# Experts taken by the rank of their counts, one set of split weights for both parts, and routing in larger groups

## The chip, the cores and the metric

The kernel runs on one core of one Trainium2 chip. The metric is the device time in microseconds (us) of one execution; the times of an unchanged kernel are the median of a few runs, lowest and highest beside it.

## What is computed

Three stages follow one another on 3,072 tokens of 384 values (4 sequences of 768, 8 heads of 48):

```
scan:  S_re, S_im = a * S + k v^T  (complex gate a, |a| < 1);  y[t] = q[t] S_re
moe:   logits = x @ w_gate + softplus(x @ w_noise) * noise          # 8 experts
       top2 of the logits, shares = softmax over the two
       out[token] += share * relu(x[token] @ w1[e]) @ w2[e]          # w1 384x1024, w2 1024x384
mlp:   h = max(x @ u1, x @ u2, x @ u3);  out = h @ w_out             # u 384x768, w_out 768x384
```

Inputs and outputs are float32. How many tokens an expert gets depends on the inputs; the mean is 2 x 3,072 / 8 = 768.

## The kernel before, in words

**Scan.** The tokens are 24 chunks of 128, in 6 levels of time step with one chunk of each of the 4 sequences. For each chunk PE builds scores (L732), DVE multiplies them with a mask (L736, two products a chunk), PE makes the chunk's output and state (L750, L753, L771), and the gating matmuls (L809) give the logits. A chunk's output is kept as two float16 halves (`xhl`).

**Routing.** `route()` (L822 on) takes the chunks in 12 groups of 2 (`groups` in the table `P`, L43). For a group DVE finds the two best experts of each token (L844 to L866), PE and DVE turn one-hot rows into a slot in the expert's list (L882 to L900), POOL adds up the counts (L870), and four small instructions make the softmax shares (L907 to L916). Then POOL scatters the chunk's rows, one indirect DMA for each chunk and choice (L940, each with a one-element memset ahead of it, L939), into `xs_rows`, where every expert has a region of its own.

**Experts.** An expert's weights come from memory in 7 pieces (3 of w1, 4 of w2) and are split into float16 high and low halves, the high one on ACT (L985), the low one on DVE (L987), so that three float16 matmuls stand for one in float32. Each expert is done twice. The first pass (L1023 on; matmuls L1037 and L1057) takes its first 384 rows, which come from the first 12 chunks, so that it can run while the scan is still going on; `bump` (L1197) pads every expert's count to 384 there. The second pass (L1076 on; matmuls L1098, L1124) takes rows 384 to 816 (`CAP` = 816), which is three tiles of 128 rows and one of 48; the tile of 48 is done as pairs of half tiles (L1131). The first passes go through experts 0 to 7, the second ones back from 7 to 0, and only expert 7 uses the same split weights in both, so weights are fetched and split 15 times. Results go to `ys_rows` and, of the first pass, to `yf_rows` too. Rows past 816 of an expert would be done by a block under a condition at run time (L1442 on).

**Final stage.** The rows of a token's two experts are gathered by indirect DMA (L1507), weighed and added (L1513), and go through the last three-way layer (L1557) and the output layer (L1583). The first tokens' combination starts earlier, from `yf_rows` (`combine_first`, L1340 on; gathers L1351, transposes L1376 and its neighbours).

**What sets the order.** All work up to the final stage is entered into a list scheduler, `Order` (L68 on), with for each operation its engines and cost, what it reads and writes, the buffers it holds, and a due time (chunk or part number plus a value of the table `o`, L36 on). Its greedy loop writes all instructions out in the order that it finds, so a change of a cost or of a number in `o` can move any instruction. SP issues the loads, the transposing loads of the experts' rows (L1006, one for each 128 columns of a half), the weight pieces (L997) and the writes of results (L1069, L1152). On every engine instructions run in the order in which they stand.

Of the kernel before, what the change touches and what calls it, by code (L numbers as in the profile page):

```python
# [22 lines left out]
SX = 2.0 ** 5  # L23
# [12 lines left out]
    o=dict(load=-278.44, e1=-80.82, g=-44.76, ex=27.33, lam=13.6, t1=124.93, t2=491.73, f=-344.44, sin=58.57,  # L36
           tc=-621.27, qkv=204.29, v=669.22, a0=-227.64, a=84.82, b=-227.33, d=-609.19, c=-58.23, s=-165.23,
           l=90.33, f_=14.8, rt=-247.65, scat=-246.48, zf=803.51, gate=-153.95, noise=149.71, xw=125.96, xx=-312.17,
           x1=-201.57, xe=-424.5, x2=17.72, xo=-1189.75, yw=61.09, yx=-118.02, y1=-594.47, ye=185.57, y2=-134.08,
           yo=454.95, uw=1011.11, ue=388.46, pl=276.27, z=-83.6, mr=971.2),  # L40
    sets=[4, 4, 4, 4, 4, 4],
    e1ph=[0, 1, 2, 3, 4, 5],
    groups=[2, 2, 2, 2, 2, 2, 2, 2, 2, 2, 2, 2],  # L43
# [205 lines left out]
def tile_kernel(ctx, tc, q, k, v, a_re, a_im, w_gate, w_noise, noise, w1, w2,  # L249
# [20 lines left out]

    xs = nc.dram_tensor("xs_rows", (E * NT, 2 * HD), F16).ap()

    NX = -(-((E - 2) * RA - (E * CAP - 2 * NT)) // 128) * 128
# [5 lines left out]
    zs = nc.dram_tensor("z_rows", (NT, 2 * HD), F16).ap()  # L279

# [107 lines left out]
    for nm, pool_, shape, dt in (  # L388
# [15 lines left out]
            ("rw", ck, [128, 61 * max(P["groups"])], F32),  # L404
# [415 lines left out]
    RW = (("e", E), ("nl", E), ("mx", 8), ("ix", 8), ("oh0", E), ("oh1", E), ("rb", E), ("dm", 2), ("ew", 2), ("sm", 1))  # L820

    def route(gi, i0, n):  # L822
# [6 lines left out]
        def pr(x=0):  # L829
            return i0 + n - 1 + x, "rt"  # L830
# [4 lines left out]
        def oh(t):  # L835
            return d[("oh0", "oh1")[t]]()
# [22 lines left out]

        def r1b5(e_):  # L860
            for t in range(2):
                nc.vector.tensor_tensor(oh(t), b3(iota8), exf[:, sl_][:, :, t:t + 1].to_broadcast([128, n, E]),
                                        op=OP.is_equal)

        def r1b6(e_):
            nc.vector.tensor_tensor(a16[:, sl_], oh(0), oh(1), op=OP.add)  # L866
# [5 lines left out]
        def r1d(e_):  # L872
            mx = d["mx"]()
            nc.vector.tensor_tensor(d["dm"](), mx[:, :, :2], mx[:, :, 0:1].to_broadcast([128, n, 2]), op=OP.subtract)
# [3 lines left out]
        def rps():  # L878
            return tl("ps", ("r", i0))[:, :B * E].rearrange("p (n e) -> p n e", e=E)[:, :n]
# [11 lines left out]
        def r2b1(e_):  # L891
            for t in range(2):
                nc.vector.tensor_tensor(oh(t), oh(t), d["rb"](), op=OP.mult)

        def r2b2(e_):
            for t in range(2):
                nc.vector.tensor_reduce(slf[:, sl_, t], oh(t), axis=AX.X, op=OP.add)
# [3 lines left out]

        def r3(e_):
            act(d["ew"](), d["dm"](), AF.Exp)

        def r3b(e_):
            ew = d["ew"]()
            nc.vector.tensor_tensor(d["sm"](), ew[:, :, 0:1], ew[:, :, 1:2], op=OP.add)  # L907

        def r3c(e_):
            nc.vector.tensor_scalar(d["sm"](), d["sm"](), 1e-9, None, op0=OP.add)  # L910

        def r3d(e_):
            nc.vector.reciprocal(d["sm"](), d["sm"]())

        def r3e(e_):
            nc.vector.scalar_tensor_tensor(wt[:, sl_], d["ew"](), SZ / (SX * SW * SW),  # L916
                                           d["sm"]().to_broadcast([128, n, 2]), op0=OP.mult, op1=OP.mult)
# [5 lines left out]
        O.add(r1, {"ACT": 0.4}, pr(), r=ky("zl"), w=[("rw", i0, 0)], table=0)  # L923
        for m, (f, c) in enumerate(((r1b, 0.1), (r1b1, 0.1), (r1b2, 0.1 * n), (r1b3, 0.14 * n), (r1b4, 0.08), (r1b5, 0.2),
                                    (r1b6, 0.1))):
            O.add(f, {"DVE": c}, pr(), r=[("rw", i0, m), ("nz", 0, None)], w=[("rw", i0, m + 1)], two=m in (0, 1, 5, 6))
        O.add(r2, {"PE": 0.06 + 0.03 * n * (n + 1) // 2}, pr(), r=[("acc", slot[gi], None), ("rw", i0, 7)], w=[pp_])
        O.add(r1c, {"POOL": 0.2 * n}, pr(), r=[("acc", slot[gi], None), ("rw", i0, 7)], w=[("acc", slot[gi] + 1, None)], two=True)
        O.add(r1d, {"DVE": 0.08}, pr(1), r=[("rw", i0, 3)], w=[("rv", i0, "d")], hold=[("rw", i0)], two=True)
        O.add(r2b, {"DVE": 0.1}, pr(), r=[pp_], w=[("rw", i0, 8)])  # L930
        for m, (f, c) in enumerate(((r2b1, 0.2), (r2b2, 0.2), (r2b3, 0.08))):
            O.add(f, {"DVE": c}, pr(), r=[("rw", i0, m + 8)], w=[("sl", i0, None) if m == 2 else ("rw", i0, m + 9)], two=m == 0)
        O.add(r3, {"ACT": 0.1}, pr(1), r=[("rv", i0, "d")], w=[("rv", i0, 0)], hold=[("rw", i0)], table=0)
        for m, f in enumerate((r3b, r3c, r3d, r3e)):
            O.add(f, {"DVE": 0.08}, pr(1), r=[("rv", i0, m)], w=[("rv", i0, m + 1)], hold=[("rw", i0)], two=m in (0, 3))
# [15 lines left out]
        for j in range(n):  # L951
            for t in range(2):
                O.add(scatter(i0 + j, t), {"POOL": 1.26}, (i0 + j, "scat"),
                      r=[("sl", i0, None), ("xhl", i0 + j, None)] + [("xz", e, None) for e in range(E)], w=[("xs", i0 + j, t)], xfer=0.27)
# [677 lines left out]
```

## Time and profile before

| what | before |
|---|---|
| time, median of 3 runs | 984.25 us (978.99 to 984.77) |
| profiled execution, first to last instruction | 983.5 us |
| PE busy, matmuls | 930.6 us, 6,312 |
| weight loads of PE | 586.8 us, 6,312 |
| DVE busy | 574.0 us, 1,252 instructions |
| ACT busy | 476.0 us, 922 |
| POOL busy | 139.0 us, 197 |
| moved by DMA | 150.98 MB |

The profiled execution's own time is its span, 983.5 us, 0.75 us below the median of the runs. PE is TensorE, PEld its weight loads, which overlap matmuls, DVE is VectorE, ACT ScalarE, POOL GpSimd, SP the engine that issues DMAs. A busy share is a mean over stages with different limits, so the windows (busy time by stretches of time) and the groups (busy time by line of the code and shape) have to be read together. In a window's row the columns are the stretch, its length, busy us and instructions of PE, PEld, DVE, ACT and POOL, the granted clock of PE as a share of full speed, the DMA engines' share, and GB/s. In a group's row they are line, engine, operation, output and inputs, shape, count, then busy us and mean ns of one, then idle us ahead of it and what ended that.

### The profile page before, as it was taken

What the parts mean: (1) busy time and instruction counts of PE and PEld (TensorE: products, weight loads), DVE (VectorE), ACT (ScalarE), POOL (GpSimd) and SP (SyncE); (2) the same over time, 40 slices, a digit from 0 to 9 for tenths busy, and PEclk for the clock granted to TensorE, in tenths of its full rate; (3) what the DMA queues carried; (4) which work ended last, traced back from release to release, by engine and by line L of the source; (5) the groups of instructions that cost most, each with busy time, mean ns of one, the idle gap of its engine ahead of it and who ended that gap; (6) DMA issues with size and microseconds to landing.
All of it is one profiled execution on the core that took longest, in us unless ns stands there. A gap on an engine that the chain in (4) does not pass through costs nothing. (4 is left out here: it accounts for less than half of the span.)

```text
span 983.5 us, 16814 instructions
## 1 busy us (share of the span) xinstructions
PE 930.6 (95%) x6312; PEld 586.8 (60%) x6312; DVE 574.0 (58%) x1252; ACT 476.0 (48%) x922; POOL 139.0 (14%) x197
## 2 busy tenths in 40 slices
PE   3989778899999999899999999999799999999998
PEld 1868667787666766455555555555675445454544
DVE  5989748999655756565887764454344332424231
ACT  7998748978644556243445444333233132313221
POOL 0101442422001000520100000000433030300000
PEclk9999969999999999899999999999999999999999
DMA  9999848796765546379888785552335141502000
GB/s 150 211 214 271 195 120 159 182 194 165 191 185 168 158 153 201 123 223 312 253 253 238 209 208 155 147 141 79 107 116 142 40 133 36 140 25 78 25 9 33
DMA packets 247902, 150.98 MB, mean 154 GB/s; under 512 B 196488, under 2 KB 235528, under 8 KB 247816
## 3 DMA queue, kind: packets, MB, share of 16 engines
q1 hardware_dynamic: 241672, 130.98, 52.1%
q0 software_dynamic: 6144, 18.88, 6.4%
q8 instruction: 50, 0.82, 0.4%
q14 instruction: 36, 0.29, 0.1%
HBM read 89.78 MB, written 45.81 MB: 138 GB/s over the span
## 5 line engine op out<-in xcount | busy, mean ns | idle before, releaser
L437 ACT ACTIVATE hh<-bk 128x384 f16<-128x384 f32 (+1 forms) x128 | 64.6, 508 | 85.4 <-PE bk L1098 43.2
L985 ACT ACTIVATE w<-wst 128x768 f16<-128x768 f32 (+1 forms) x77 | 71.1, 932 | 59.6 <-PE bk L1057 23.3
L1057 PE MATMUL bk<-w,hh 128*128 128x384 f16 x576 | 98.6, 331 | 1.3 <-issue 1.3
L1037 PE MATMUL bk<-xa,w 128*128 128x384 f16 x576 | 99.6, 326 | 0.0
L987 DVE SCALAR_TENSOR_TENSOR w<-wst,w 128x768 f16<-128x768 f32 (+1 forms) x77 | 81.4, 1068 | 12.4 <-ACT w L985 11.5
L1571 ACT ACTIVATE th<-mx 128x512 f16<-128x512 f32 (+1 forms) x42 | 23.8, 568 | 127.2 <-DVE mx L1570 125.5
L1057 PEld LDWEIGHTS <-hh 128*128 128x128 f16 x576 | 56.7, 99 | 41.6 <-issue 6.5
L1124 PEld LDWEIGHTS <-hh 128*128 128x128 f16 x576 | 55.0, 98 | 40.3 <-issue 5.0
L1037 PEld LDWEIGHTS <-w 128*128 128x128 f16 x576 | 55.1, 98 | 34.4 <-issue 1.4
L1569 DVE TENSOR_TENSOR mx<-mx,u 128x512 f32<-128x512 f32 (+1 forms) x42 | 25.6, 610 | 62.5 <-PE u L1557 62.5
L1507 POOL DMA_INDIRECT yg<-ys_rows,sy x42 | 43.5, 1036 | 119.6 <-ACT za L1511 104.4
L940 POOL DMA_INDIRECT xs_rows<-xhl,sl x48 | 55.4, 1154 | 35.5 <-issue 18.5
L443 DVE COPY ya<-bk 128x384 f32<-128x384 f32 x37 | 20.6, 558 | 67.7 <-PE bk L1057 45.7
L732 PE MATMUL sc<-qt,kt 96*128 96x128 f32 x384 | 55.4, 287 | 4.5 <-issue 1.8
L732 PEld LDWEIGHTS sc<-qt,kt 96*128 96x128 f32 x384 | 49.3, 197 | 12.1 <-issue 4.1
L1098 PE MATMUL bk<-xa,w1b 128*128 128x432 f16 x288 | 53.2, 346 | 0.0
L1098 PE MATMUL bk<-xa,w 128*128 128x432 f16 x288 | 53.2, 346 | 0.0
L1107 DVE SCALAR_TENSOR_TENSOR hh<-bk,hh 128x432 f16<-128x432 f32 x64 | 37.9, 605 | 24.9 <-ACT hh L437 24.8
L1124 PE MATMUL bk<-w2b,hh 128*128 128x384 f16 x288 | 48.4, 326 | 0.0
L1124 PE MATMUL bk<-w,hh 128*128 128x384 f16 x288 | 48.4, 326 | 0.0
L1570 DVE TENSOR_TENSOR mx<-mx,u 128x512 f32<-128x512 f32 (+1 forms) x42 | 25.7, 611 | 37.4 <-PE u L1557 33.2
L1513 DVE SCALAR_TENSOR_TENSOR z<-yg,wt,za 128x384 f32<-128x384 f32 x22 | 12.8, 614 | 58.7 <-ACT za L1511 52.2
(204 smaller groups left out, 2012.7 us busy)
## 6 DMA issues: line engine op xcount, KB each, us to landing
wst<-in_moe_w_dram SPq DMA_DIRECT2D x45, 512.0 KB
wst<-in_moe_w_dram SPq DMA_DIRECT2D x60, 384.0 KB
xs_rows<-wst SPq DMA_DIRECT2D x8, 1152.0 KB
ys_rows<-ya SPq DMA_DIRECT2D x48, 192.0 KB
raw<-in_moe_w_dram SPq DMA_DIRECT2D x9, 768.0 KB
ar<-in_a_re_dram SPq DMA_DIRECT2D x24, 192.0 KB
ai<-in_a_im_dram SPq DMA_DIRECT2D x24, 192.0 KB
q<-in_q_dram SPq DMA_DIRECT2D x24, 192.0 KB
```

Of the source, the lines that this page charges most:

```text
L437: nc.scalar.activation(o, i, f, **kw)
L732: nc.tensor.matmul(tl("sc", (i, g))[:, j, :], tl("kt", i)[:, h, :], tl("qt", i)[:, h, :], start=True, stop=True)
L940: ins = nc.gpsimd.indirect_dma_start(out=xs, out_offset=bass.IndirectOffsetOnAxis(ap=sl[:, i, t:t + 1], axis=0), in_=tl("xhl", i), in_offs ...
L985: nc.scalar.activation(hi, src, AF.Copy, scale=scale)
L987: nc.vector.scalar_tensor_tensor(lo, src, scale, hi, op0=OP.mult, op1=OP.subtract)
L1037: nc.tensor.matmul(tl(*b)[:, :RA], tl("w1", e)[:, w, k, f * 128:(f + 1) * 128], tl("xa", e)[:, x + k, :RA], start=(k == m == 0), stop=(k = ...
L1057: nc.tensor.matmul(tl(*b)[:, :HD], tl("hh", e)[:, a, f, t * 128:(t + 1) * 128], tl("w2", e)[:, w, f], start=(f == m == 0), stop=(f == KF - ...
L1098: nc.tensor.matmul(tl(*b)[:, :RB], tl(n1, inst)[:, w, k, f * 128:(f + 1) * 128], tl("xa", xi)[:, x + k], start=(k == m == 0), stop=(k == K ...
L1107: nc.vector.scalar_tensor_tensor(tl("hh", xi)[:, 1, f], tl(*b)[:, :RB], 0.0, tl("hh", xi)[:, 0, f], op0=OP.max, op1=OP.subtract)
L1124: nc.tensor.matmul(tl(*b)[:, :HD], tl("hh", xi)[:, a, f, ts_], tl(n2, inst)[:, w, f], start=(f == m == 0), stop=(f == KF - 1 and m == 2))
L1507: nc.gpsimd.indirect_dma_start(out=y, out_offset=None, in_=src, in_offset=bass.IndirectOffsetOnAxis(ap=row[:, i, s:s + 1], axis=0))
L1570: nc.vector.tensor_tensor(a, a, ps[2], op=OP.max)
```

## The change

- Experts are no longer all given 816 rows in a fixed order. Experts 0 and 1 (`NF = 2`) keep 816 rows and their place. When all counts are known, the other six are ordered by their counts, and the n-th of them in that order has room for 816, 784, 768, 768, 768 and 768 rows (`CAPS`). The rank is worked out by some ten DVE instructions (`p_1`); six loads on SP take it into registers (`p_er`), and the weights, rows and results of a ranked expert are then addressed through its register (`of(n)`).
- `first_pass` and `second_pass` become one function, `expert(n, part, at, fresh)`. Order: first parts of 0 and 1, second part of 1, then both parts of each ranked expert one behind the other on the same split weights, then the second part of 0. Weights are fetched and split 9 times. `bump` pads only experts 0 and 1.
- A ranked expert's part with fewer rows than 816 writes zero rows over the rest of its region (`f_n`).
- The check for overflowing rows compares with the limit by rank (`p_caps`).
- Routing takes groups of 4, 4, 4, 4, 4, 2 and 2 chunks. Instructions for the first and second choice are put in one, with twice the columns. The softmax of the shares is done once for all chunks behind the last group (`shares`).
- All numbers of the table `o` are others; the planner's costs of the routing instructions are too.

```
-    groups=[2, 2, 2, 2, 2, 2, 2, 2, 2, 2, 2, 2],
+    groups=[4, 4, 4, 4, 4, 2, 2],
...
-    o=dict(load=-278.44, e1=-80.82, ...
+    o=dict(a=-2647.32, a0=-19905.55, ...
...
+    NF = 2
+    CAPS = [CAP] * NF + [816, 784, 768, 768, 768, 768]
+    ER = {}
+    def of(n):
+        return slice(n, n + 1) if n < NF else bass.ds(ER[n], 1)
...
         def r1b5(e_):
-            for t in range(2):
-                nc.vector.tensor_tensor(oh(t), b3(iota8), exf[:, sl_][:, :, t:t + 1].to_broadcast([128, n, E]),
-                                        op=OP.is_equal)
+            nc.vector.tensor_tensor(ohs().rearrange("p n t e -> p (n t) e"), iota8[:, None, :].to_broadcast([128, 2 * n, E]),
+                                    two(exf)[:, :, None].to_broadcast([128, 2 * n, E]), op=OP.is_equal)
...
         def r2b2(e_):
-            for t in range(2):
-                nc.vector.tensor_reduce(slf[:, sl_, t], oh(t), axis=AX.X, op=OP.add)
+            nc.vector.tensor_reduce(two(slf), ohs().rearrange("p n t e -> p (n t) e"), axis=AX.X, op=OP.add)
...
-        def r3(e_):
-            act(d["ew"](), d["dm"](), AF.Exp)
...
+    def shares():
+        def w0(e_):
+            act(wt, dmx, AF.Exp)
+        def w1_(e_):
+            nc.vector.tensor_tensor(sm, wt[:, :, 0], wt[:, :, 1], op=OP.add)
...
     def load_rows(e, t, lo, hi, j):
-        return nc.sync.dma_start_transpose(t[:, j, :hi - lo], xs[e * NT + lo:e * NT + hi, j * 128:(j + 1) * 128])
+        return nc.sync.dma_start_transpose(t[:, j, :hi - lo],
+                                           xs3[of(e), lo:hi, j * 128:(j + 1) * 128].rearrange("o n d -> (o n) d"))
...
-    def first_pass(e):
+    def expert(n, part, at, fresh):
+        lo = RA * part
+        rows = CAPS[n] - RA if part else RA
+        early = n < NF and not part
+        inst = (n, part) if fresh else (n, 0)
...
+            if part and t == nt - 1 and CAPS[n] < CAP:
+                def f_n(e_, y=y):
+                    nc.sync.dma_start(ys3[of(n), CAPS[n]:].rearrange("o n d -> (o n) d"), tl(*y)[:CAP - CAPS[n]])
...
         def p_1(e_):
             cnt = Q["cnt"]
             nc.vector.tensor_copy(cnt, tl(*ps)[:, :E])
-            nc.vector.tensor_scalar(Q["ovf"], cnt, float(-CAP), 0.0, op0=OP.add, op1=OP.max)
-            nc.vector.tensor_reduce(Q["nbi"], Q["ovf"], axis=AX.X, op=OP.max)
+            key, rank, c2 = Q["key"], Q["rank"], Q["ohr"].rearrange("p (a b) -> p a b", b=E)
+            nc.vector.scalar_tensor_tensor(key, cnt, float(2 * E), iota8, op0=OP.mult, op1=OP.subtract)
+            nc.vector.memset(key[:, 0:NF], -1.0)
+            nc.vector.tensor_tensor(c2, key[:, None, :].to_broadcast([128, E, E]), key[:, :, None].to_broadcast([128, E, E]), op=OP.is_gt)
+            nc.vector.tensor_reduce(rank, c2, axis=AX.X, op=OP.add)
...
+        def p_er(n):
+            def f(e_):
+                ER[n] = nc.values_load(Q["ordi"][0:1, n - NF:n - NF + 1], engines=[mybir.EngineType.SP], min_val=0, max_val=E - 1,
```

The order of the instructions shows it at three places. The first is DVE in the scan, at the routing of one group among the chunks' work (`rw` is the group's scratch tile, `pm` the masked scores, `a` the one-hot sums, `xt` and `zp` tiles of the scan). Before, a group of 2:

```order
L851 MAX rw_838<-rw_838 128x8 x2
L855 MAX_INDEX rw_838<-rw_838 128x8 x2
L874 TENSOR_TENSOR rw_838<-rw_838 128x4
L858 CAST exf<-rw_838 128x4
L862 TENSOR_TENSOR rw_838<-iota_85,exf 128x16 x2
L907 TENSOR_TENSOR rw_838<-rw_838 128x2
L736 TENSOR_TENSOR pm_379<-sc_339,mask 128x512
L866 TENSOR_TENSOR a_139<-rw_838 128x16
L910 TENSOR_SCALAR rw_838<-rw_838 128x2
```

Now, a group of 4:

```order
L749 TENSOR_TENSOR pm_365<-sc_344,mask 128x512
L877 TENSOR_TENSOR rw_979<-iota_85,exf 128x64
L1005 SCALAR_TENSOR_TENSOR w_2486<-wst_162,w_2486 128x768
L881 TENSOR_TENSOR a_139<-rw_979 128x32
L1005 SCALAR_TENSOR_TENSOR w_2486<-wst_1777,w_2486 128x768
L749 TENSOR_TENSOR pm_397<-sc_344,mask 128x512
L904 TENSOR_TENSOR rw_979<-ps_387,basee 128x32
L1005 SCALAR_TENSOR_TENSOR w_2486<-wst_1839,w_2486 128x768
L907 TENSOR_TENSOR rw_979<-rw_979 128x64
L808 TENSOR_REDUCE zp_577<-bk_212 128x16
```

The instructions have twice to four times the columns, the softmax instructions (L907, L910 of before) are gone from here, and weight pieces of the first expert stand between.

The second is POOL, at a group's scatters (`acc` are the counts, `xhl` the chunks' rows, `mb` and `tn` tiles of the scan). Before:

```order
L870 TENSOR_TENSOR acc<-acc,a_139 128x8 x2
L513 TENSOR_TENSOR tn_168<-ai_157,iv_166 128x384
L939 MEMSET spacer 1x1
L940 DMA xs_rows<-xhl_640,sl 24576x768
...
L940 DMA xs_rows<-xhl_712,sl 24576x768
...
L870 TENSOR_TENSOR acc<-acc,a_139 128x8 x2
L783 TENSOR_TENSOR mb_113<-mb_113,lx_1292 96x8x48
```

Now:

```order
L885 TENSOR_TENSOR acc<-acc,a_139 128x8 x4
L935 MEMSET spacer 1x1
L936 DMA xs_rows<-xhl_972,sl 24576x768
...
L936 DMA xs_rows<-xhl_1072,sl 24576x768
...
L936 DMA xs_rows<-xhl_1120,sl 24576x768
...
L936 DMA xs_rows<-xhl_1256,sl 24576x768
...
L796 TENSOR_TENSOR mb_113<-mb_113,lx_747 96x8x48
```

Four scatters of two chunks stood between additions; now eight of four chunks stand in a row behind one addition. The last three groups' scatters, 16, stand with only two additions between them.

The third is SP, among the loads for the experts (`wst` is a piece of weights, `xa` an expert's rows, transposed). Before:

```order
L997 DMA wst_1904<-in_moe_w_dram 128x2x384
L1006 DMA_TRANSPOSE xa_2146<-xs_rows 128x384
L1069 DMA ys_rows<-ya_2811 128x384
L1069 DMA yf_rows<-ya_2811 128x384
L997 DMA wst_160<-in_moe_w_dram 128x2x384
L1006 DMA_TRANSPOSE xa_2146<-xs_rows 128x384
L997 DMA wst_1803<-in_moe_w_dram 128x1024
L1006 DMA_TRANSPOSE xa_2146<-xs_rows 128x384
```

Now, a ranked expert, with pieces of the final stage's weights (`raw`) between:

```order
L1015 ISA
L1015 DMA wst_1894<-in_moe_w_dram 128x1024
L1024 ISA
L1024 DMA_TRANSPOSE xa_2315<-xs_rows 128x432
L1127 DMA ys_rows<-ya_3279 128x384
L1156 DMA raw_3328<-in_moe_w_out_dram 128x768
L1015 ISA
L1015 DMA wst_162<-in_moe_w_dram 128x1024
L1024 ISA
L1024 DMA_TRANSPOSE xa_2315<-xs_rows 128x432
```

Each load through a register has an instruction for its address (ISA) ahead of it, 170 in all.

## Rows read from the trace of the kernel before

**Rows 1.** The page: span, PE's busy time, and scatters (busy, mean ns, idle before).
```profile
span 983.5 us, 16814 instructions
...
PE 930.6 (95%) x6312; PEld 586.8 (60%) x6312; DVE 574.0 (58%) x1252; ACT 476.0 (48%) x922; POOL 139.0 (14%) x197
...
L940 POOL DMA_INDIRECT xs_rows<-xhl,sl x48 | 55.4, 1154 | 35.5 <-issue 18.5
```

**Rows 2.** Windows, all engines: stretch, length, busy us (count) each, clock, DMA share, GB/s.
```profile
0.00:50.00 50.00, 33.37 (x238) 24.77 (x239) 37.10 (x95) 42.70 (x89) 4.82 (x12) 1.00 1.08 184
...
100.00:150.00 50.00, 38.98 (x305) 32.46 (x300) 31.62 (x89) 32.67 (x71) 22.23 (x35) 0.80 0.64 156
150.00:200.00 50.00, 43.75 (x444) 37.12 (x443) 45.89 (x131) 44.33 (x98) 18.38 (x23) 0.97 0.76 167
...
400.00:450.00 50.00, 45.52 (x286) 26.53 (x285) 25.73 (x67) 15.03 (x26) 15.89 (x32) 0.93 0.68 199
```

**Rows 3.** Windows, all engines, either side of 235.5 us.
```profile
157.00:235.50 78.50, 70.40 (x707) 59.43 (x706) 73.32 (x204) 68.19 (x145) 27.70 (x40) 0.98 0.87 183
235.50:429.00 193.50, 189.88 (x1366) 124.75 (x1365) 120.17 (x271) 97.17 (x177) 22.37 (x40) 0.98 0.59 171
```

**Rows 4.** Windows of the mask products (L736, DVE) alone.
```profile
0.00:235.50 235.50, 25.93 (x38) 0.94 0.90 189
163.80:213.90 50.10, 5.43 (x8) 0.97 0.80 172
```

**Rows 5.** Windows, all engines, in and behind runs of scatters.
```profile
121.50:130.50 9.00, 4.35 (x15) 2.40 (x15) 0.16 (x1) 2.33 (x6) 7.47 (x16) 0.73 0.48 174
130.50:144.00 13.50, 11.15 (x80) 10.15 (x79) 7.74 (x24) 6.58 (x15) 4.21 (x10) 0.55 0.20 60
238.40:243.80 5.40, 5.40 (x39) 3.63 (x38) 4.58 (x9) 4.35 (x11) 4.75 (x7) 1.00 0.42 135
...
402.30:412.80 10.50, 7.07 (x24) 3.06 (x25) 3.65 (x8) 0.45 (x1) 8.58 (x17) 0.67 0.58 191
```

**Rows 6.** Windows of the scatters (L940, POOL) alone.
```profile
115.00:121.50 6.50, 5.28 (x5) 1.00 0.61 161
121.50:130.50 9.00, 6.78 (x8) 0.73 0.48 174
...
402.30:412.80 10.50, 7.62 (x8) 0.67 0.58 191
```

**Rows 7.** Groups of PE by shape: busy us, mean ns, idle before.
```profile
L1037 PE MATMUL bk<-xa,w 128*128 128x384 f16 x576 | 99.6, 326 | 0.0
L1057 PE MATMUL bk<-w,hh 128*128 128x384 f16 x576 | 98.6, 331 | 1.3 <-issue 1.3
...
L1098 PE MATMUL bk<-xa,w1b 128*128 128x432 f16 x288 | 53.2, 346 | 0.0
...
L1124 PE MATMUL bk<-w2b,hh 128*128 128x384 f16 x288 | 48.4, 326 | 0.0
...
L1131 PE MATMUL bk<-w2b,hh 128*48 128x384 f16 x96 | 9.3, 329 | 0.0
```

**Rows 8.** Groups of DVE by shape: a weight split, a routing instruction.
```profile
L987 DVE SCALAR_TENSOR_TENSOR w<-wst,w 128x768 f16<-128x768 f32 x44 | 41.3, 953 | 7.8 <-ACT w L985 6.9
...
L893 DVE TENSOR_TENSOR rw<-rw 128x16 f32<-128x16 f32 x24 | 3.0, 166 | 0.1
```

**Rows 9.** The chain of waits between experts and final stage: start, us, what.
```profile
689.64 0.99 POOLq L1447
...
691.01 0.04 POOLq L1507
```

**Rows 10.** SP's issues by tile: count, then ns min/median/max, first and last start.
```profile
L1006 SPq DMA_TRANSPOSE xa<-xs_rows x96: 1112/1132/2422, 197.3 to 641.8; - x96
...
L997 SPq DMA_DIRECT2D wst<-in_moe_w_dram x105: 333/512/2066, 161.9 to 663.5; - x105
...
L1069 SPq DMA_DIRECT2D yf_rows<-ya x24: 422/424/1478, 254.8 to 470.6; - x24
```

More of the change, by code (lines that the diff above doesn't have):

```diff
@@ L1024, in f_x @@
                 def f_x(e_, j=z * KD + k):
-                    ins = load_rows(e, tl("xa", e), 0, RA, j)
-                    for o in later:
-                        tc.declare_no_dep(ins.ins, o.ins, reason="the second pass's rows begin after the first's")
-                    loads.append(ins)
-                load(f_x, pr("xx"), [("xa", e, (k, z))], xfer=0.65,
-                     r=[("xs", i, None) for i in range(NA)], row="xa")
+                    ins = load_rows(n, tl("xa", xi), lo, lo + rows, j)
+                    if early:
+                        for o in later:
+                            tc.declare_no_dep(ins.ins, o.ins, reason="the second part's rows begin after the first's")
+                        loads.append(ins)
+                load(f_x, pr("xx"), [("xa", xi, (k, z))], xfer=0.75 if rows > RA else 0.65,
+                     r=[("xs", i, None) for i in range(NA if early else NI)] + ([("er", n, None)] if n >= NF else []), row="xa")
         for f in range(KF):
-            b = ("g", (e, 1, f))
+            b = ("g", (n, 1 + 2 * part, f))
             prev = None
@@ L1117, in second_pass @@
+            O.add(f_h, en(["act"], rows, True), pr("xe"), r=[b + (None,)], w=[("hh", xi, (f, 0))], hold=slots(b))
+            O.add(f_l, en(["dve"], rows), pr("xe"), r=[b + (None,), ("hh", xi, (f, 0))], w=[("hh", xi, (f, 1))], hold=slots(b))
+        nt, nr = divmod(rows, 128)
+        assert nr <= 64
+        for t in ([nt] if nr else []) + list(range(nt)):
+            b = ("g", (n, 2 + 2 * part, t))
+            prev = None
             ts_ = slice(t * 128, t * 128 + (nr if t == nt else 128))
@@ L1216, in bump @@
         O.add(f_3, {"DVE": 0.08}, pr, r=[("more", 0, 0)], w=[("more", 0, 1)])
-        O.add(f_4, {"DVE": 0.08}, pr, r=[("more", 0, 1), ("acc", GA, None)], w=[("acc", GA + 1, None)], two=True)
+        O.add(f_4, {"DVE": 0.16}, pr, r=[("more", 0, 1), ("acc", GA, None)], w=[("acc", GA + 1, None)], two=True)
     NB = 52
@@ L1406, in tile_kernel @@
     before = len(O.ops)
-    for e in range(E):
-        first_pass(e)
     wp = ExitStack()
     O.add(swap, {"SP": 0.01}, (NI, "pl"), w=[("swap", 0, None)], after=range(before))
-    for n in range(E):
-        second_pass(n)
+    shares()
     place_rows()
+    parts = [(0, 0, True), (1, 0, True), (1, 1, False)] + [(n, part, not part) for n in range(NF, E) for part in range(2)] + [(0, 1, True)]
+    for at, (n, part, fresh) in enumerate(parts):
+        expert(n, part, at, fresh)
     before = len(O.ops)
```

245 lines of the change are left out of this document (116 added, 129 removed).

## The prediction

> **What bounds the kernel now.** I read the page first: PE is busy for 930.6 of 983.5 us [rows 1], so time can only come from PE work that goes or from the 52.9 us in which PE stands still. The second view, windows of 50 us, says where those lie [rows 2]: 16.6 us in the first window, 11.0 and 6.3 from 100 to 200 and 4.5 from 400 to 450, that is 38.4 of the 52.9. So the experts' stage is bound by PE alone, and the scan with its routing, most of which lies in the first 250 us, is bound by something else. The third view, two windows either side of 235.5, names it [rows 3]: between 157.0 and 235.5 DVE is busy for 73.3 of 78.5 us (93%) and PE for 70.4 (90%), while from there to 429 PE has 98% and DVE 62%. Counting the mask products (two for each chunk, 48 in all), 38 lie ahead of 235.5 [rows 4], so 19 chunks run at DVE's pace, and the last five lie spread under the experts' matmuls. The fourth view is of the scatters [rows 5, 6]: behind the start of a run of twelve without a break, eight scatters come in 9.0 us in which PE is busy for only 4.35 and DVE for 0.16, at a clock of 0.73; a second such run has 7.07 of 10.5 us at 0.67; a run of four (238.4 to 243.8) has PE busy throughout at 1.00. The first long run's five scatters ahead of 121.5 [rows 6] took 6.5 us; so both long runs stop all engines from about the sixth scatter on, and lower the clock.
>
> **PE work that goes.** Four of the eight second parts shrink from 432 to 384 rows and lose the tile of 48 rows: its 192 matmuls in eight experts take 2 x 9.3 us [rows 7], 2.33 us an expert, so 4 x 2.33 = 9.3 us. Their 72 first-layer matmuls fall from 53.2/288 = 184.7 ns to the 48.4/288 = 168.0 ns of a 384-column matmul in the same stage: 4 x 72 x 16.7 ns = 4.8 us. The expert with 400 rows loses 32 of the 48 columns, 72 x 16.7 x 32/48 = 0.8 us. All of it is on the path, PE being full there: **-14.9 us**. This needs no unknown cost.
>
> **First parts out of the scan.** First-part matmuls take (99.6 + 98.6)/1152 = 172.0 ns where second-part ones of the same width take 168.0: 4.6 us in all, at lower clock between the scan's instructions. Six of eight first parts now follow the scan. Bounds 0 and -4.6, I take **-2**.
>
> **Weights split 9 times, not 15.** Each split is 3 pieces of 1,024 columns and 4 of 768, 4 x 0.953 us for the latter [rows 8] and as much again for the former, some 7.5 us of DVE, the same on ACT, and 7 fetches. Five of the six that go lie where PE is full and DVE not, and I cost them at nothing; ahead of the 38th mask product two single pieces fewer remain (5 for 7).
>
> **Routing in larger groups.** Ahead of the 38th mask product DVE issues 68 routing instructions where it issued 159. The small ones take 166 ns [rows 8] and grow with the columns in the wide form, so 91 fewer are worth at most 91 x 0.166 = 15 us less what the wider ones add; a small instruction is nearly all fixed cost, so I put that at 3 us, and add the two splits, 2 x 0.95. At most 14 us, if DVE alone sets the pace; nothing, if the order merely lets other DVE work slide in, or if larger groups make the scatters late. PE's own 90% there leaves only 8.1 us in this window. I take **-6**.
>
> **The scan's tail.** The order shows the last five chunks with only 42 first-layer matmuls of the first expert between them, where in the kernel before they lay under eight first parts. At 12.5 us a chunk (8 mask products in 50.1 us [rows 4]) these would take 62.6 us; their PE work is at most 12.5 x 0.90 = 11.3 us a chunk, 56 us, which counts the gate products of later levels that are over by then; I estimate 50 us, of which the fillers are 42 x 0.172 = 7.2. At 0.98 busy that is 51 us, at 0.90 it is 55.6. Since DVE has fewer routing instructions there too, I take half of the difference, **+2**, with bounds 0 and 62.6 - 51 = +11.6.
>
> **Scatters in runs of 8, 8, 8, 8 and 16.** A stall from the sixth on makes 7 + 7 = 14 stalled scatters before, and 4 x 3 + 11 = 23 now, 9 more. By idle time alone (3.43 us in 7 stalled ones in the second run [rows 5, 6]) one costs 0.49 us, nine 4.4 us. By the first run, which with its half-clock stretch to 144 loses 4.65 us idle, 2.35 more, and some 6 us of speed (11.15 us of work at 0.55), 13.0/7 = 1.86 us each, nine cost 16.7 us. If runs of eight do not stall, 11 are left for 14, -2.5 us. I take **+4**: the run at the scan's end has expert matmuls to fill it, like the second. A new wait is in this run: the last group's two count additions stand on POOL behind twelve of its scatters, and PE's count matmul, nine matmuls (1.5 us) behind that group's routing, waits for them, with all expert matmuls queued behind it. The eight scatters of the group before the last two come while DVE still has some 40 instructions to do for the last group, so I cost it at nothing, with four scatters, 4 x 1.15 [rows 1] = 4.6 us, as the other end.
>
> **Rank chain and dynamic addresses.** Behind the last routing come the count matmul, some ten DVE instructions of 0.17 us, six register loads on SP, and then the weights of expert 2 by rank. A register load with its branch takes 0.99 us on POOL's queue [rows 9], six 5.9 us. The order leaves 3 + 4 x 72 matmuls of 384 columns at 0.168 or 0.172 us and the 432-column part of expert 1, together some 64 us, before the first one that needs them; 2 + 6 + 15 us (3.07 MB at the 199 GB/s of 400 to 450 [rows 2]) + 8 us of splits is 31, so this is hidden with 33 us to spare. The dynamic issues are the unknown: 170 of SP's DMAs, 28 an expert, get an address instruction. A register step ahead of a gather takes 0.04 us on POOL's queue, the load 0.99 [rows 9]; between these I take a small fraction, since it is register arithmetic. SP's own work is 12 transposes at 1.13, 7 fetches at 0.51 and 9 or 10 writes at up to 0.42 us [rows 10] = 21 us an expert against the 50 us of PE that 288 matmuls of 0.168 and the gaps between stages make. What is queued behind an issue on SP is the next expert's weights and rows, a part ahead. I take **+2** for both, bounds 0 and +10 below the point where SP becomes the bound. The four transposes of the combine that now come behind the last expert matmul, at most 0.33 us each, add **+1.5** with the wait for the first. The softmax of all chunks is one activation and four DVE instructions behind the last routing, first read by the combine behind most expert matmuls, and four fewer writes of zero rows lie under full PE: nothing.
>
> **Sum.** -14.9 - 2 - 6 + 2 + 4 + 2 + 1.5 = -13.4 us on the profiled 983.5, 970.1; the median of the runs is 0.75 above that span, so **971**.
>
> **Rivals.** *A: long scatter runs stop everything.* For it: both runs of twelve [rows 5]. Against: a run of four leaves PE at 1.00, and expert matmuls stand behind the scan's end. Price: 16.7 in place of 4, 971 + 12.7 = 984. [...] 0.14.
>
> *B: the tail runs at DVE's pace.* Five chunks without cover take 62.6 us, 11.6 in place of 2. For it: 93% DVE in [rows 3]. Against: 91 fewer instructions. 971 + 9.6 = 981. 0.13.
>
> *C: SP becomes the bound (slower).* If one dynamic issue costs over (50 - 21)/28.3 = 1.02 us, SP needs more than the 50 us that PE takes for an expert, and each of the six ranked experts waits for rows and weights. At 1.2 us it is 21 + 28.3 x 1.2 = 55 us, 6 x 5 = 30 us more: 1001. For it: 0.99 us for a register load on another queue. Against: 0.04 us for plain register work there. 0.12.
>
> *D: the change does not do what it says.* A count above its smaller limit runs the block for overflowing rows at run time. The gating of the reference on its inputs gives counts 767, 794, 774, 757, 804, 762, 755, 731; the six ranked are 804, 774, 762, 757, 755, 731 against limits 816, 784 and 768, so all fit. Should one not, another 3.07 MB of weights (15 us) and some 10 us of work follow: 996. 0.04.
>
> **Numbers.** Forecast 0.57. One per cent is 9.8 us, about what can be told from no change: faster below 974.4, slower above 994.1. The forecast's own spread puts 0.52 of its chance on faster and 0.05 on same; A and B are same, 0.27; C and D slower, 0.16. Range: downward all of the 14 us of DVE (8 more), of the 4.6 us (2.6) and the scatters' -2.5 (6.5) would give 954, and since they hardly come together I set 956; upward it takes in A and B, and A with 8 us of dynamic issues, 992; C and D stay out.
>
> **What would show it.** Right: PE busy some 15 us lower in sum; 96 matmuls of the half-tile form instead of 192 and 72 of 400 columns; PE full from the scan's end to the last expert, with every dynamic DMA issued ahead of use; the 38th mask product earlier than 235.5. Wrong: PE idle at the start of each ranked expert with SP named (C); windows of low PE and half clock around each run of eight scatters (A); a last stretch of the scan with DVE above 90% and PE below 85% (B); a block for overflow in the trace (D). What would overthrow the sum is a stall in the experts' stage, where I cost all fetches at nothing.

## The result and the profile after

The changed kernel takes 971.65 us (median of 4 runs, 968.36 to 975.05), the kernel before 983.5 us beside it (4 runs); the ratio is 0.9883 with a 95% interval of 0.985 to 0.9915. The forecast was 971, faster by 1.3%. The profiled execution spans 968.6 us where that of before spans 983.5 [rows 1], 14.9 us less.

The page of the kernel after gives the span and PE's busy time:

```profile
span 968.6 us, 16631 instructions
...
PE 912.0 (94%) x6231; PEld 581.4 (60%) x6231; DVE 522.0 (54%) x1095; ACT 433.9 (45%) x849; POOL 139.8 (14%) x201
```

PE's work fell by 930.6 - 912.0 = 18.6 us, and its idle time rose from 52.9 to 56.6 us. Where the idle time lies is read from windows. The first is cut at the same time in both and not at the same place of the program, since the kernel after is 8.8 us ahead there; the others are cut where the scan and the experts end. First the kernel before, by stretch, length, busy us and instructions of PE, PEld, DVE, ACT, POOL, clock, DMA share, GB/s; the stretch from 235.5 to 429 stands in [rows 3]:

```profile
0.00:235.50 235.50, 196.70 (x1780) 162.38 (x1781) 192.46 (x556) 193.66 (x421) 60.96 (x98) 0.94 0.90 189
...
429.00:650.00 221.00, 220.14 (x1360) 123.42 (x1358) 146.84 (x233) 96.02 (x155) 10.29 (x15) 1.00 0.75 219
650.00:983.50 333.50, 323.88 (x1812) 176.27 (x1810) 114.56 (x194) 89.18 (x170) 45.42 (x44) 0.99 0.26 75
```

Then the kernel after, whose scan ends at about 300:

```profile
0.00:235.50 235.50, 201.77 (x1871) 166.18 (x1871) 196.67 (x497) 202.72 (x431) 63.08 (x102) 0.96 0.80 186
235.50:300.00 64.50, 53.31 (x495) 42.54 (x495) 40.86 (x124) 29.72 (x60) 26.76 (x51) 0.89 0.35 104
300.00:650.00 350.00, 347.70 (x2145) 205.39 (x2144) 178.79 (x290) 118.36 (x196) 4.65 (x6) 1.00 0.55 162
650.00:968.60 318.60, 309.26 (x1725) 167.32 (x1723) 105.70 (x184) 83.13 (x163) 45.31 (x44) 0.99 0.24 70
```

PE's idle time in the scan up to 235.5 falls from 38.8 to 33.7 us; the scan's tail has 11.2 us where the stretch of before has 3.6; the experts have 2.3 where they had 0.9; the end 9.3 where it had 9.6. The tail is where most was lost, at a clock of 0.89, and the experts lost 1.4 us. The experts' groups after (busy us, mean ns of one; before in [rows 7]):

```profile
L1073 PE MATMUL bk<-xa,w 128*128 128x384 f16 x504 | 85.8, 328 | 0.0
...
L1073 PE MATMUL bk<-xa,w1b 128*128 128x384 f16 x360 | 59.3, 326 | 0.0
...
L1073 PE MATMUL bk<-xa,w1b 128*128 128x432 f16 x144 | 26.6, 346 | 0.0
...
L1073 PE MATMUL bk<-xa,w 128*128 128x400 f16 x72 | 12.3, 332 | 0.0
...
L1106 PE MATMUL bk<-w2b,hh 128*48 128x384 f16 x48 | 4.6, 329 | 0.0
```

864 first-layer matmuls have 384 columns now. The 360 on `w1b` all lie in the experts' own stage and take 59.3/360 = 164.7 ns each, the 504 on `w`, some of them between the scan's, 170.2; those with 432 keep 184.7.

The scatters' windows, which answer to [rows 5]: three of the five runs of eight, and a run of four. The last sixteen came as 8, 4 and 4, with breaks of 2.9 and 8.6 us between them.

```profile
186.00:196.50 10.50, 6.92 (x64) 4.87 (x63) 4.67 (x11) 7.59 (x16) 9.05 (x15) 0.90 0.88 245
230.30:240.20 9.90, 7.49 (x58) 5.42 (x52) 4.44 (x8) 4.54 (x10) 8.53 (x15) 0.93 0.99 221
268.30:278.90 10.60, 6.91 (x69) 5.17 (x68) 3.99 (x20) 1.59 (x5) 8.70 (x18) 0.88 0.35 131
295.10:300.40 5.30, 5.30 (x34) 3.22 (x33) 3.05 (x4) 1.58 (x3) 4.64 (x8) 1.00 0.71 230
```

PE stands for 2.4 to 3.7 us in each of these runs of eight and not at all in the run of four, so runs of eight do stall. What PE waits for there, from the waits of PE between 20 and 450 us (us in all, times, longest), is named "issue": nothing that the profile shows.

```profile
PE ps L784 <- issue: 5.5, 5, 2.0
PE bk L822 <- issue: 3.7, 1, 3.7
```

All rows of that name make 13.4 us there, against 9.4 in the kernel before, whose timeline of PE in its first run of twelve scatters shows what they are (start, duration, idle time ahead in brackets):

```profile
122.30 0.34 PE L753 MATMUL py<-qt,mb 96*64 96x128 f32 x2 [1.08 <-issue]
123.73 0.27 PE L753 MATMUL py<-qt,mb 96*64 96x128 f32 x1 [1.09 <-issue]
123.93 0.38 PE L732 MATMUL sc<-qt,kt 96*128 96x128 f32 x1
125.18 0.36 PE L732 MATMUL sc<-qt,kt 96*128 96x128 f32 x1 [0.87 <-issue]
125.89 0.37 PE L732 MATMUL sc<-qt,kt 96*128 96x128 f32 x1 [0.35 <-issue]
```

PE gets on with one small matmul in 0.7 to 1.4 us though the profile names nothing that it waits for. ACT and DVE stand longer still: their next instructions in that run start at 132.48, behind single waits of 7.8 and 8.8 us, and both read what PE had written by 124.0. The profile calls these waits "remote", a releaser that it cannot place. The same shows in the tail of the kernel after, in its run from 268.3 on:

```profile
276.28 0.60 ACT L454 ACTIVATE xt<-py 128x512 f16<-128x512 f32 x1 [6.10 <-remote]
276.35 0.17 DVE L904 TENSOR_TENSOR rw<-ps,basee 128x16 f32<-128x16 f32 x1 [4.87 <-remote]
276.94 0.61 PE L822 MATMUL bk<-wgn,xt 128*128 128x128 f16 x4 [3.69 <-issue]
```

So PE's issue waits are not the whole of the stall. In the tail they make 7.1 of its 11.2 us, and 1.9 more are a wait of PE for ACT's `xt`, which had itself stood at "remote" for 3.7 us. The granted clock of the tail is 0.89, with 11.2 us of standing in 64.5: it reads 0.50 from 239.2 to 248.9 us and from 277.0 to 279.7, behind the starts of the stalls at 237.2 and 273.2, and 0.99 to 1.00 in the windows from 249.1 to 276.7 and from 280 on.

### The profile page after: what moved, and what is told of

Its sections match the earlier page's. It is cut to its first block, busy times and chain, and to the rows that moved or that the text cites. A ratio compares the mean times of both kernels' runs of the same rounds, so it can differ in the third digit from the quotient of the medians.

```text
span 968.6 us, 16631 instructions
## 1 busy us (share of the span) xinstructions
PE 912.0 (94%) x6231; PEld 581.4 (60%) x6231; DVE 522.0 (54%) x1095; ACT 433.9 (45%) x849; POOL 139.8 (14%) x201
## 5 line engine op out<-in xcount | busy, mean ns | idle before, releaser
L450 ACT ACTIVATE hh<-bk 128x384 f16<-128x384 f32 (+2 forms) x128 | 63.2, 497 | 155.4 <-PE bk L1073 154.1
L1073 PE MATMUL bk<-xa,w 128*128 128x384 f16 (+2 forms) x648 | 111.5, 331 | 0.0
L1099 PE MATMUL bk<-w,hh 128*128 128x384 f16 x648 | 107.5, 326 | 2.3 <-DVE w L1005 1.9
L1083 DVE SCALAR_TENSOR_TENSOR hh<-bk,hh 128x384 f16<-128x384 f32 (+2 forms) x128 | 71.2, 565 | 68.9 <-ACT hh L450 68.8
L1073 PE MATMUL bk<-xa,w1b 128*128 128x384 f16 (+1 forms) x504 | 85.9, 332 | 0.0
L1099 PE MATMUL bk<-w2b,hh 128*128 128x384 f16 x504 | 83.4, 326 | 0.0
L1073 PEld LDWEIGHTS <-w1b 128*128 128x128 f16 x504 | 49.3, 98 | 35.3
L1585 DVE TENSOR_TENSOR mx<-mx,u 128x512 f32<-128x512 f32 (+1 forms) x42 | 25.6, 609 | 65.5 <-PE u L1573 59.3
L1599 PE MATMUL o<-woh,th 128*128 128x384 f16 x144 | 46.9, 326 | 0.0
L1599 PE MATMUL o<-wol,th 128*128 128x384 f16 x144 | 46.9, 326 | 0.0
L1599 PE MATMUL o<-woh,tl 128*128 128x384 f16 x144 | 46.9, 326 | 0.0
```

The lines of the kernel that those rows point to most:

```text
L450: nc.scalar.activation(o, i, f, **kw)
L1073: nc.tensor.matmul(tl(*b)[:, :rows], tl(n1, inst)[:, w, k, f * 128:(f + 1) * 128], tl("xa", xi)[:, x + k, :rows], start=(k == m == 0), sto ...
L1083: nc.vector.scalar_tensor_tensor(tl("hh", xi)[:, 1, f, :rows], tl(*b)[:, :rows], 0.0, tl("hh", xi)[:, 0, f, :rows], op0=OP.max, op1=OP.sub ...
L1099: nc.tensor.matmul(tl(*b)[:, :HD], tl("hh", xi)[:, a, f, ts_], tl(n2, inst)[:, w, f], start=(f == m == 0), stop=(f == KF - 1 and m == 2))
L1585: nc.vector.tensor_tensor(a, a, ps[1], op=OP.max)
L1599: nc.tensor.matmul(p, a[:, f, ts_], w[:, f], start=(m == 0), stop=(m == 3 * KU - 1))
```

## The experiments

Two things have to be known to read them. The kernel before took 957.13 us in the first set, on one chip, and 982 to 983 us in the three others, on three other chips, so kernels are compared within a set, by ratios to it. And in the first set's four profiles PE has no wait named issue at all between 20 and 450 us, nor DVE or ACT one named remote, with the same scatters; that set shows the kernel without the stall. The changed kernel itself was not run in it; the kernel with fixed addresses stands in for it there.

**816 rows for all ranked experts.**
```
-    CAPS = [CAP] * NF + [816, 784, 768, 768, 768, 768]
+    CAPS = [CAP] * E
```
Expected: 

> The changed kernel with 816 rows for all six ranked experts too (limits by rank taken away, rank and register addresses kept); the scan's instructions stay as they are. Sum of the prediction: the four tiles of 48 rows and the 432-column matmuls come back, PE busy 912.0 + 14.9 = 927 us, PE's idle time as it was (56.6 us), time 971.65 + 14.9 = 986.5. Rival, the gain came from the fewer splits and the new order: time within 3 us of 971.65.

Measured: 962.44 us, ratio 1.0066 (1.0045 to 1.0086); against the kernel with fixed addresses in the same set 19.0 us slower. PE busy, with fixed addresses and with 816 rows:

```profile
PE 901.1 (96%) x6231; PEld 576.6 (61%) x6231; DVE 524.8 (56%) x1095; ACT 434.2 (46%) x849; POOL 145.7 (15%) x201
PE 919.0 (96%) x6327; PEld 582.1 (61%) x6327; DVE 528.1 (55%) x1096; ACT 436.1 (45%) x850; POOL 145.0 (15%) x201
```

Of the groups, the two of the half tiles:

```profile
L1106 PE MATMUL bk<-w2b,hh 128*48 128x384 f16 x96 | 9.3, 329 | 0.0
L1106 PE MATMUL bk<-w,hh 128*48 128x384 f16 x96 | 9.3, 329 | 0.0
```

The half tiles are back with 9.4 us, first-layer matmuls with 6.9, the unchanged second-layer ones with 1.1, and PE's busy time with 17.9 us in all. With 816 rows the kernel is slower than the one before, so the smaller limits are worth more than the whole gain, here 13.7 us, and the rival, that splits and order brought it, falls. The 19.0 us also hold what register addresses cost, since only one of the two kernels has them.

**Fixed addresses.**
```
+    BY = {2: 4, 3: 2, 4: 5, 5: 3, 6: 6, 7: 7}
...
-        return slice(n, n + 1) if n < NF else bass.ds(ER[n], 1)
+        return slice(n, n + 1) if n < NF else slice(BY[n], BY[n] + 1)
```
Expected: 

> The changed kernel with the ranked experts' weights, rows and results at fixed addresses, in the order that these inputs' counts give (4, 2, 5, 3, 6, 7); the rank is still worked out and loaded, and waited for, but no DMA uses it. It serves these inputs only. Prediction: the dynamic issues lie under 50 us of PE an expert and cost 0 to 2 us, so 969.7 to 971.7, with PE full in the experts' stage as before. Rival C: SP sets part of the experts' time, over 5 us faster, under 967.

Measured: 943.41 us, ratio 0.987 (0.9849 to 0.9891), the ratio that the changed kernel has in its own sets. What it shows by itself is where PE stands from 300 to 650: 1.3 us here, 2.3 in the changed kernel, all of them waits for weight splits and none for SP:

```profile
PE bk L1099 <- DVE w L1005: 1.9, 1, 1.9
PE bk L1099 <- ACT w L1003: 0.4, 1, 0.4
```

SP's issues of weight pieces, first with registers (the kernel after), then fixed (ns least/median/most):

```profile
L1015 SPq DMA_DIRECT2D wst<-in_moe_w_dram x63: 342/406/1310, 148.7 to 596.5; - x63
L1015 SPq MOVE wst<-in_moe_w_dram x42: 29/29/40, 317.1 to 549.8; - x42
```
```profile
L1016 SPq DMA_DIRECT2D wst<-in_moe_w_dram x63: 370/442/1404, 146.0 to 575.9; - x63
```

A register shows as a move of 29 ns, and the issue itself is no dearer, 406 ns at the median for 442. Rival C, which needed 1.02 us an issue and PE standing in the experts' stage, falls.

**96 more small DVE instructions in the scan.**
```
+    dum = const.tile([128, E], F32, name="dum")
...
             def f_m(e, g=g):
+                for _ in range(2):
+                    nc.vector.tensor_tensor(dum, iota8, iota8, op=OP.mult)
                 nc.vector.tensor_tensor(tl("pm", (i, g)), tl("sc", (i, g)), ...
```
Expected: 

> The changed kernel with two small DVE instructions (128x8) more ahead of each of the 48 mask products, 76 of them ahead of the 38th product, order unchanged otherwise. They stand for the routing instructions that the change took out of the scan. Prediction: DVE sets the pace there in part; 91 fewer gave 6 us, so 76 to 96 more cost about 5 us: 977. Rival 1, DVE sets the pace all along: 96 x 0.166 = 16 us, 987. Rival 2, the routing's instructions cost nothing: 971.65 within 1.

Measured: 954.2 us, ratio 0.997 (0.9956 to 0.9985), 10.8 us over the kernel with fixed addresses; its page:

```profile
PE 904.0 (95%) x6231; PEld 576.8 (61%) x6231; DVE 538.2 (57%) x1192; ACT 436.4 (46%) x849; POOL 143.8 (15%) x201
```

DVE has 13.4 us more than the 524.8 of the fixed-address kernel, and the span is 8.4 us longer (949.6 for 941.2): between the 5 us of the forecast and the 16 us of full pace. How much of it is the scan's shows where the 48th, the last mask product stands (stretch, length, DVE's us on mask products and their count, clock, DMA share, GB/s), with fixed addresses and then with the 96 instructions:

```profile
0.00:265.50 265.50, 32.77 (x48) 0.97 0.77 181
0.00:265.50 265.50, 31.23 (x46) 0.97 0.85 177
0.00:273.00 273.00, 32.83 (x48) 0.97 0.83 176
```

It ends at 265.3 and at 272.7 us, and at 266.7 in the kernel with 816 rows, which has register addresses too: 6.0 to 7.4 us later for 13.4 us of DVE. So DVE sets the scan's pace for about half of its time.

**15 splits in the new order, and the splits' engine time alone.**
```
-        swapped = n >= NF and n % 2 == 0 or n < NF and fresh and part
+        swapped = not early and at % 2 == 1
...
-    parts = ... [(n, part, not part) for n in range(NF, E) for part in range(2)] ...
+    parts = ... [(n, part, True) for n in range(NF, E) for part in range(2)] ...
```
Expected: 

> The changed kernel with weights fetched and split anew for both parts of each ranked expert, 15 times in all, in two sets of buffers by turns as in the kernel before; everything ahead of the ranked experts is unchanged. Prediction: six splits more lie under full PE and cost nothing, 971.65 within 2, DVE +45 us and ACT +40 us busy, DMA +19 MB. Rival, the shared weights were worth something of their own: over 4 us slower, with PE waiting for weights at the second parts.

Measured: 995.63 us, ratio 1.041 (1.0388 to 1.0431), 52 us slower than the fixed-address kernel. The prediction that six splits more cost nothing fails; the rival had the sign and the wait, but not the size. PE stands for 28.4 us between 300 and 650 and waits for splits, here the two longest of its waits:

```profile
PE bk L1073 <- ACT w L1003: 9.9, 4, 3.3
PE bk L1073 <- ACT w1b L1003: 8.4, 2, 4.2
```

```
-                    O.add(lambda e_, ...: halves(e_, tl(*st), tl(tag, inst)), ...
+                    O.add(lambda e_, ...: [halves(e_, tl(*st), tl(tag, inst)) for _ in range(2 if inst[0] >= NF else 1)], ...
```
Expected: 

> The changed kernel with each weight piece of the six ranked experts split twice over on ACT and DVE (same result, order and transfers unchanged): the engines' time of the six splits that the change saved, without their fetches and buffers. Splitting 15 times with fetches cost some 50 us in this order. If that was the engines' time, 20 us and more slower; if it was the fetches, for which one part's 25 us leave little room, within 3 us of the changed kernel.

Measured: 983.28 us, ratio 1.0001 (0.9976 to 1.0026), 12 to 15 us over the changed kernel, between the two expectations. PE's idle time from 300 to 650 is 14.2 us, and it waits for evictions on DVE, which is busy for 217.0 us there where it was for 178.8:

```profile
PE bk L1073 <- DVE hh L1083: 4.7, 3, 2.8
```

So the engines' time matters, and the fetches with their buffers seem to matter more, when they are put where the planner had not reckoned with them; the two runs belong to different sets. Neither says that the six splits cost anything in the kernel before, where PE is full from 429 to 650. They say that the new order, with both parts of an expert back to back, has no room for six splits more.

**Scatters further apart.** First the changed kernel and the kernel before again on one chip: the changed kernel 966.89 us, ratio 0.985 (0.9821 to 0.988), issue waits 10.3 us; the kernel before, its one run, 981.74 us, 9.3.
Expected of the changed kernel: 

> The changed kernel itself once more, beside the kernel before on the same chip, since the kernel before took 957 us in the last comparison where it took 984 earlier. If the gain is PE work (14.9 us) with small terms about it, the ratio stays at 0.988, a gain of 11 to 13 us. Rival, the gain hung on stalls of that one chip: ratio within 0.005 of 1, or below 0.98.

Expected of the kernel before: 

> The kernel before once more, for its profile on this chip. If the time of 957 comes from fewer stalls in the scan, PE is busy for nearly 1.00 in the two runs of twelve scatters and its idle time falls from 52.9 us to under 45; if the chip is faster in all, the final stage is shorter too.

The stall is in both, with PE at 0.62 and 0.82 busy in the two runs of twelve of the kernel before, and the ratio holds with it as without it (0.985 here, 0.987 in the first set), so the gain does not hang on it.

```
-    spacer = const.tile([1, 1], F32, name="spacer")
+    spacer = const.tile([128, 384], F32, name="spacer")
...
-                nc.gpsimd.memset(spacer, 0.0)
+                for _ in range(3):
+                    nc.gpsimd.memset(spacer, 0.0)
```
Expected: 

> The changed kernel with three memsets of 128x384 (0.42 us each) ahead of each scatter in place of one of one element: scatters come every 2.5 us in place of 1.27, order unchanged. Forecast's price: the runs of 8 and 16 lose some 4 us against unstalled ones, and later scatters cost little: 4 us faster to 2 slower than the changed kernel. Rival A, runs of eight and more stall all engines by their density: 12 to 20 us faster. Third theory, the stalls do not come from the density: no stall is gone, and the longer runs delay the rows, 0 to 10 us slower.

Expected of the kernel before with the same edit: 

> The kernel before with the same three memsets ahead of each scatter. By rival A's price the two runs of twelve lose 13.0 + 5.8 us, so 12 to 19 us faster where they stall, the gaps of 6.8 us on DVE and 10 us on ACT gone. If density is not the cause: within 3 us of the kernel before, or slower.

Measured: changed kernel 990.14 us, ratio 1.0074 (1.0045 to 1.0104); kernel before 982.2, ratio 0.9996 (0.9972 to 1.002). The changed kernel is 23 us slower than unspaced, outside all three expectations, and the kernel before is where it was. The issue waits are gone, 0.5 and 0.3 us for 10.3 and 9.3, and so are the remote waits of DVE and ACT between 20 and 450 us: on this chip the stall comes with the density of the scatters. But other waits take more than they gave back. The waits of PE in the spaced changed kernel:

```profile
PE ps L1241 <- POOL acc L885: 12.5, 1, 12.5
PE bk L734 <- ACT kt L454: 8.2, 3, 7.2
...
PE py L766 <- POOL mb L796: 3.1, 1, 3.1
```

The first is the wait that the prediction named behind the last group's count additions and costed at nothing; stretched twice over it is 12.5 us. In the changed kernel it does not show.

**Groups of 2, and a smaller space.** In all three kernels due times were searched anew, since those of the change were made for its groups; what the search itself gave is not separated. The changed kernel was not run beside them.
```
-    o=dict(a=-2647.32, a0=-19905.55, ...
+    o=dict(a=-2876.05, a0=-33048.14, ...
...
-    groups=[4, 4, 4, 4, 4, 2, 2],
+    groups=[2, 2, 2, 2, 2, 2, 2, 2, 2, 2, 2, 2],
```
Expected: 

> The changed kernel with routing in 12 groups of 2 chunks as before (paired instructions and the softmax at the end kept), the planner's due times searched anew for it, since the change's own were made for the large groups. By the prediction's terms the larger groups gave -6 on DVE and cost +4 in scatter runs, so their net is about 2 us: 0 to 4 us slower than the changed kernel, beside which the ratio to the kernel before was 0.985 to 0.988. Rival A, runs of 8 and 16 scatters cost much: runs become shorter, 5 to 12 us faster than the changed kernel. Rival B, DVE sets the pace all along: 8 us and more slower.

Measured: 962.81 us, ratio 0.9793 (0.9773 to 0.9813), issue waits 3.8 us. By the ratios that is 6 to 9 us faster than the changed kernel, where the forecast had 0 to 4 us slower. Rival A had the sign, but the stall did not get less. PE waits for ACT's `xt` here, and ACT stands at "remote" ahead of each of these three waits:

```profile
PE bk L822 <- ACT xt L454: 7.2, 3, 4.1
ACT xt L454 <- remote: 12.0, 3, 6.4
```

With the issue waits that is 11.0 us. The kernel with double splits, which has the changed kernel's scatters and ran in this set, has 5.7 us of issue waits and 4.5 of such waits for `xt`, 10.2 together. So the gain of this kernel lies in the groups or in the new order, and not in a shorter stall.

One memset of 128x384 (0.42 us) ahead of each scatter, and the last two groups' count additions on DVE:
Expected: 

> The changed kernel with one memset of 128x384 (0.42 us) ahead of each scatter, so one every 1.7 us, the count additions of the last two groups on DVE so that no wait for them stands behind scatters, and due times searched anew for it. With 2.5 us between scatters the waits of PE that the profile calls issue fell from 10.3 to 0.5 us, and waits behind POOL took more than that. If 1.7 us suffice and the waits behind POOL are gone: issue waits under 3 us, 5 to 12 us faster than the changed kernel (ratio 0.973 to 0.980). If the stall needs more space to go: issue waits as they were, 0 to 5 us slower.

Measured: 963.5 us, ratio 0.9784 (0.9756 to 0.9811), issue waits 0.2 us, as expected if so small a space suffices, and PE is busy for 64.44 of 64.5 us in the tail.

Groups of 2 and that one memset together:
Expected: 

> The changed kernel with groups of 2 chunks and one memset of 128x384 ahead of each scatter together, due times searched anew. If the two act on one thing, the stall of PE's issue in long scatter runs, they don't add: ratio 0.976 to 0.981 to the kernel before, as each alone (0.979 and 0.978), issue waits under 1 us. If groups of 2 gave something else besides, they add: 0.970 to 0.975.

Measured: 953.02 us, ratio 0.9694 (0.9674 to 0.9714), 30 us under the kernel before. They add: the space took the stall, with issue waits of 0.2 us and no remote wait of DVE or ACT up to 450 us, and groups of 2, or the search that came with them, gave something else. Its windows:

```profile
235.50:300.00 64.50, 62.59 (x549) 45.93 (x546) 52.46 (x166) 31.93 (x65) 36.69 (x52) 1.00 0.52 166
300.00:650.00 350.00, 346.31 (x2135) 202.85 (x2135) 169.07 (x259) 115.71 (x193) 3.84 (x4) 1.00 0.52 147
```

The tail that stood for 11.2 us at a clock of 0.89 now stands for 1.9 at 1.00.

## Why the prediction was right, step by step

**PE work that goes, -14.9.** Right in kind, somewhat low. By the run with 816 rows the limits are worth 17.4 us in the experts' own groups and 17.9 in PE's busy time. The half tiles gave 9.4 us for 9.3. The first layer gave 6.9 for 5.6, since the 168.0 ns were read from second-layer matmuls, and first-layer ones of that width take 164.7.

**First parts out of the scan, -2 of at most -4.6.** Not shown. PE's busy time fell by 18.6 us, and by 15.9 (927.0 to 911.1) in the second pair of profiles, the kernels run again on one chip; less the 17.9 us of the limits this leaves 0.7 and -2.0 us for the first parts and the scan's matmuls together. The groups' rows can't size the step. One matmul lasts 326 ns where the next starts some 165 ns later, so wherever a first-part matmul stands between the scan's, the rows of both count the same time; the 172.0 ns of the estimate were read from such rows. And the bound is for all eight first parts; for the six that moved it is 3.5.

**Routing in larger groups, -6.** The size is right and the cause is not shown. PE's idle time up to 235.5 us fell by 5.1 us, and by 6.7 (39.28 to 32.54) in the second pair. The marker held: the 38th mask product ends at 226.3 us, 8.8 earlier than before, and in the second pair at 222.0 where it was 233.6. The mask products alone, in the kernel before, in the kernel after and with groups of 2:

```profile
0.00:234.00 234.00, 25.25 (x37) 0.94 0.90 188
0.00:226.50 226.50, 25.96 (x38) 0.96 0.80 186
0.00:215.00 215.00, 25.91 (x38) 1.00 0.81 197
```

But with groups of 2 that product comes earlier still, with more DVE instructions up to 235.5 us, 557 for 497, and PE stands for only 29.8 us there:

```profile
0.00:235.50 235.50, 205.69 (x1962) 168.84 (x1963) 206.52 (x557) 207.67 (x450) 72.99 (x109) 1.00 0.80 196
```

So the fall need not come from the larger groups. The pairing of the instructions, the softmax at the end, the two splits fewer and the new order are left as causes, and no run tells them apart. The 96 instructions show that DVE has a say of about half. The small instructions themselves took 151 ns at 128x8 (L889), 184 at 128x32 (L857) and 219 to 229 at 128x64 (L877, L907) in the kernel after, so most of the time of one does not go with its columns.

**Tail +2 and scatters +4.** PE's idle time in the tail is 7.6 us above the stretch from 235.5 to 429 of before, and 4.6 (7.6 for 3.0) in the second pair, for 6 forecast. The split between the two was wrong: without the stall (first set, fixed addresses) the tail stands for only 0.9 us (63.62 of 64.5), so nearly all of it is the scatters. Rival B falls: PE is below its 85% in the tail, with 53.31 of 64.5 us, but DVE has 40.86, far from 90%. Rival A was right that runs of eight stall, and its price was too high: issue waits rose by 4.0 and 1.0 us and PE's idle time in the tail by 7.6 and 4.6, for the 16.7 of its price. Its count of 23 stalled scatters took the last sixteen for one run, and they came as 8, 4 and 4. Its price also has a slip: 11.15 us of work at a clock of 0.55 lose, by the estimate that time goes with the clock, 5.0 us and not some 6, so nine scatters would cost 15.4 (in the kernel before a matmul of L750 took 429 ns on the mean from 130.5 to 142 us, at a clock of 0.50, and 278 from 144 to 157, at 1.00); and the -2.5 us for runs of eight that do not stall follow from neither price, since three scatters fewer are -1.5 or -5.6. The granted clock of the tail is 0.89, behind 11.2 us of standing, and 1.00 with fixed addresses, behind 0.9.

**Rank chain and dynamic addresses, +2.** PE stands 1.4 us more in the experts' stage, where 1.9 of its 2.3 us are one wait for a weight split; the addresses show as 29 ns each, and no wait of PE there names SP.

**Transposes at the end, +1.5.** Not seen: 9.3 us of idle time from 650 on, for 9.6.

**Splits at nothing.** It held in the kernel after, where PE stands for 2.3 us in the experts' stage, but no run took the splits out of the kernel before.

**Sum.** PE work -18.6 for -16.9, idle time +3.7 for +3.5: -14.9 for -13.4. In the second pair it is -15.9 and -0.7, together -16.6. The mechanism of the main term, PE work that goes where PE is full, was right and needed no unknown cost. That the median came within a microsecond of 971 is luck: the same kernel took 966.89 us when it was run again, and the smaller terms, some too high and some too low, partly cancel.

## What to carry to other kernels

Where one engine is full for a stage, count its instructions by shape: work taken off it there was worth its whole duration here (17.9 us of PE's busy time, 19.0 of the kernel's), and that term should carry the forecast. Rows of groups that overlap don't add up; the engine's busy time does. Work costed at nothing is hidden by an order, not by its nature; the same six splits cost 12 to 52 us in an order that did not expect them. An engine that is off the critical path can still hold up the others by how densely it issues: the same 48 scatters, in dense runs of up to eight or with a small space between them, together with groups of 2 and their order, made 14 to 19 us of difference between two kernels whose PE work is not far apart (906.6 and 912.0 us). And a stall can hide behind another engine's name: in the kernel with groups of 2 most of it stands in PE's list as a wait for ACT (7.2 of 11.0 us).

## What the runs showed of the hardware

Dense indirect scatters of POOL, one in 1.27 us, held PE's issue to one matmul in 0.7 to 1.4 us with no wait shown, mostly from the fifth or sixth of a run on; DVE and ACT stood with them, in single waits of 1.6 to 10.3 us named remote, each ahead of an instruction that reads what PE wrote. With one scatter in 1.7 or 2.5 us these waits are gone (issue waits 0.2 to 0.5 us for 9.3 to 13.4). In the first set of runs the same dense scatters stalled nothing, a run of twelve with PE busy throughout, as these windows of the fixed-address kernel show:

```profile
257.20:265.00 7.80, 7.80 (x85) 6.23 (x84) 6.30 (x28) 3.13 (x8) 6.30 (x13) 1.00 0.33 122
265.00:272.90 7.90, 7.90 (x75) 5.40 (x74) 4.68 (x19) 2.96 (x8) 6.59 (x13) 1.00 0.42 157
```

There the kernel before took 957 us and not 983, and no profile of it was taken there. What differs between the two stays open. So does what the scatters hold up, the start of PE's instructions or the passing on of its completions. The author's estimate from the rows of the tail is the second: the last matmul that writes `py` ended by 272.06, ACT's read of it started at 276.28, and PE's matmul at 276.94 followed ACT's end at 276.88. No run here separates the two.
